# Where the first weights are made: moving early work between VectorE, GpSimd and the load queue in a retention and two-layer kernel

## The chip, the cores and the metric

The kernel runs on one core of a Trainium2 chip. The metric is the device time of one execution in microseconds (us). Three runs of the kernel before gave 1457.69 us as their median (1457.62 to 1459.07).

## The reference, cut to what matters

```python
# q, k, v: (8 batches, 8 heads, 576 positions, 64)
scores = matmul(q, k.T) / sqrt(64)
ret = scores * Dmat              # gamma_h ** (i - j) where i >= j, else 0
x = matmul(ret, v)               # -> x: (4608 tokens, 512)
h = maximum(maximum(x @ w1, x @ w2), x @ w3)     # 512 -> 768
x = h @ w_out                                    # 768 -> 512
h = x @ w_in                                     # 512 -> 2048
out = (h * clip(h + 3, 0, 6) / 6) @ w_out2       # 2048 -> 512
```

All matrices come in as float32; the weights are handed to the core as the bits of float64.

## The kernel before, in words

**Units.** Retention is done in 32 units, a unit being one batch and one pair of heads; it is computed in chunks of 64 positions. A unit's input is one tile `raw` (or `room`, the same tile in another pool) of 128 x 2304 floats with four sections of 576 columns: `Z0`, `Z1` (queries and keys transposed), `VS1`, `VS0` (values and keys of the two heads). The first eight units (two batches) run ahead of everything else; in the program they are `us[0]` to `us[7]`, in the text units one to eight. Each goes through these steps:

- `prepare` scales the keys of section VS1 by their decay: for units one to four on ScalarE (L373) with one piece on VectorE or GpSimd (L365), from unit five on as one instruction of GpSimd (L365).
- `outers` (L382) and `scores` (L284) are matmuls of 64 x 64 blocks; a half of the array works on each head. `copied` (L399, ScalarE) and `carry` (L405) put the running state where the values can use it.
- `mask` (L426, VectorE) multiplies the scores by a table that `fill` (L351) made; there is one table per pair of heads, so four calls of `fill`.
- `values` (L320) are 16 matmuls; `values_rest` (L434, VectorE) multiplies them by the second table, and `finish` writes them as two parts, high (L333, ScalarE cast to fp32r) and low (L336, full minus high, on GpSimd or VectorE). In before, the low parts of units three to seven are not issued where they arise but put on a list `low` and issued from the loop's sixth pass on.

**Weights.** A weight tile of the first layer (24 of them, in the order `order_a`) is loaded as 128 x 512 int64 (`ws`, L100), and turned into fp32 and two fp32r parts in stages: `begin` (L113 and L114 on VectorE), `rise` (L121 and L124 on ScalarE), `join` (L132 and L134 on VectorE, then the product L136 on GpSimd; it also loads the next tile), `end` (high part, L147 on ScalarE) and `lows` (low part, L153 on VectorE). `step` does `end` of one tile, `begin` of another, `join` of a third and `lows`, in this order. Every projection `block(t, f, j)` (tokens of batch t, column tile f, matrix j) is 12 matmuls L525, L526, L527 in turn: for each of four slices of the weight tile high x high, high x low, low x high. So its first two matmuls need the tile's high part, the third its low part. `block(t, f)` without j is the second matrix of that layer.

**Order.** All is in program order per engine (`manual_schedule`): nothing is reordered, and an instruction that waits holds up all that is behind it on its engine. The eight units run in a loop in which pass i does the values of unit i+1 and the outers of the unit two further on; the steps of the weights are put between by the pass number. Then `plan` runs the blocks of the first two batches in pairs, (0,0,0), (1,0,0), (0,0,1), (1,0,1), (0,0,2), (1,0,2), (0,1,0), ..., and after each block a rule decides whether a `step` follows. Loads are issued from SyncE's queue in program order (`load_raw`, L245, two or three transfers per unit; `fetch`, L100). TensorE first runs 40 matmuls of zeros (L596), which nothing reads.

Of the kernel before, what the change touches and what calls it, by code (L numbers as in the profile page):

```python
# [37 lines left out]
def retention_moe_moe2(ctx: ExitStack, tc, raw, w_a, w_b, factors, masks, out):  # L38
# [198 lines left out]
    def load_raw(i, room=None):  # L237
        if i >= len(units) or i in raws:
            return
        b, hp = units[i]  # L240
        t = room if room is not None else at.tile([P, RAW], F32, tag="raw", bufs=3, name="raw")
        raws[i] = t

        def part(c0, c1):
            nc.sync.dma_start(out=t[:, c0:c1], in_=raw[b, hp, :, c0:c1])  # L245

        if i:
            part(VS1, RAW)
            part(Z0, VS1)
            return  # L250
        part(VS1, VS0)
        part(VS0, RAW)
        part(Z0, VS1)
# [6 lines left out]
            k = raws[i][:, VS1:VS0]  # L260
            nc.scalar.mul(k, k, kdec_sb[:, units[i][1], NC:])

    xs, low = {}, []
    banks = [ps_at.tile([P, 512], F32, name=f"at{n}") for n in range(2)]

    class Unit:
# [63 lines left out]
        def finish(self, eng=None):  # L330
            b, hp, y = self.b, self.hp, self.y
            hi, lo = xs[b][:, 0, hp, :], xs[b][:, 1, hp, :]
            nc.scalar.copy(hi, y[:, :TB])  # L333

            def rest(eng):
                eng.tensor_tensor(out=lo, in0=y[:, :TB], in1=f32(hi), op=ALU.subtract)  # L336

            if eng is low:
                low.append(lambda: rest(nc.gpsimd))
            elif eng is not None:  # L340
                rest(eng)
            else:
                late.append(lambda: rest(nc.vector))
                late.append(lambda: nc.sync.dma_start(out=xe_d[:, hp, b * C:(b + 1) * C], in_=y[:, TB:]))
# [3 lines left out]
    def fill(hp):  # L348

        for n, one in enumerate((mask_sb, qdec_sb)):  # L350
            nc.vector.tensor_tensor(  # L351
                out=tables[hp][:, n].rearrange("p (c s) -> p c s", s=C),
                in0=one[:, hp, None, :].to_broadcast([P, NC - 1, C]),
                in1=powers_sb[:, hp, n, :NC - 1, None].to_broadcast([P, NC - 1, C]), op=ALU.mult)

    class Summed(Unit):
# [75 lines left out]
        def values_rest(self):  # L432
            self.y = (rooms if self.hp % 2 else at).tile([P, S], F32, tag="yr", bufs=2, name="yr")
            nc.vector.tensor_tensor(  # L434
                out=self.y[:, :TB], in0=self.ps[1], in1=tables[self.hp][:, 1], op=ALU.mult)
            self.finish(nc.gpsimd if self.i < 2 else low if self.i < 2 * HP - 1 else nc.vector)

        def put_end(self):
            t = raws[self.i].rearrange("p (k s) -> p k s", s=S)
# [133 lines left out]
    with tc.manual_schedule():  # L573
# [6 lines left out]
        load_raw(1)  # L580
        load_raw(2, room())
        load_raw(3, room())
        wa.fetch(1)
        load_raw(4, room())
        wa.fetch(1)
        load_raw(5)
# [5 lines left out]
        pairs = [banks, spare[:2], spare[2:],  # L592
                 [ps_mm.tile([P, 512], F32, tag="mm", name="mm") for n in range(2)]]
        us = [Summed(i, pairs[i % HP if i < 2 * HP - 1 else 0]) for i in range(2 * HP)]
        for n in range(40):
            nc.tensor.matmul(spare[3][halves[n % 2], :C], lhsT=zeros[halves[n % 2], :], rhs=zeros[halves[n % 2], :],  # L596
                             start=True, stop=True)
        us[0].prepare()
        fill(0)
        fill(1)  # L600
# [1 line left out]
        us[0].all_scores()  # L602
        us[0].copied(0)
        us[1].prepare()
        us[0].join()
        us[0].mask()
        us[1].outers()
# [5 lines left out]
        us[0].values_rest()  # L613
        us[1].mask()
        us[1].join()
        fill(3)

        def block(t, f, j=None):

# [9 lines left out]
        for i, u in enumerate(us):  # L629
            one, two, three = (us[i + n] if i + n < len(us) else None for n in (1, 2, 3))  # L630
            if i:
                u.values_mm()
            u.put_end()
            if i == 0:
                load_raw(6)
            if i == 2:
                load_raw(7, room())
                wa.fetch(1)
            if one and one.i >= HP:
                one.carry()  # L640
            if three:
                three.prepare()
            if i == 0:
                ends.fill()
            if two:
                two.outers(True)
            if i:
                u.values_rest()
            begun, parts = wa.begun, wa.end() if i in (4, 6) else []
            if 1 < i < 6:  # L650
                wa.begin() if i != 4 else None
                if wa.joined < begun:
                    wa.join()
            wa.lows(parts)
            if two:
                two.copied(0)
                wa.rise()
                two.mask()
                if two.i < HP:
                    two.join()  # L660
            if i >= HP + 1:
                for n in range(2 if i < 2 * HP - 1 else len(low)):
                    low.pop(0)()
            if i == 2 * HP - 2:
                block(0, 0, 0)
        load_raw(8)
        load_raw(9)
        rooms.release()
# [10 lines left out]
        plan += [(0, f, 0), (1, f, 0), (0, f, 1), (1, f, 1), (0, f, 2), (0, f - 1), (0, f), (1, f, 2)]  # L679
        plan += [(1, g) for g in range(f)]  # L680
        decay(2 * HP)
        base = 2 * HP
        side = {(1, 1, 1): [(lambda k: ends.scores(), 0)], (1, 2, 0): [(lambda k: ends.values(), 0)],
                (1, f, 0): [(visit, 0)], (0, f, 1): [(ready, 0)], (1, f, 1): [(rest, 0)]}
        for n, (a, b) in enumerate(zip([(0, f - 1), (1, f, 2), (1, 1), (1, 3)], [(0, f), (1, 0), (1, 2), (1, 4)])):
# [2 lines left out]
        for n, blk in enumerate(plan):  # L688
            if n:
                block(*blk)  # L690
            if wa.ended < NA and n % 3 != 1 and blk != (1, 1, 1):
                wa.step()
                if wa.ended == NA - 1:
                    wb.fetch(2)
# [329 lines left out]
```

## Time and profile before

| | us |
|---|---|
| median of three runs | 1457.69 |
| the profiled execution | 1459.42 |
| its span, first to last instruction | 1457.6 |
| TensorE busy | 1442.6 |
| VectorE busy | 894.7 |

The page gives each engine's busy time over the span and in 40 slices; the timeline gives single instructions with the idle time before them and what ended it. The part of the program that the diff touches ends at some 160 us of the span; behind it the remaining batches and the second layer run with TensorE busy for nine tenths or more of every slice up to the last. The reading below is of the first 160 us.

### The profile page before, as it was taken

Reading aid. Unit: us, or ns where it says so; the run is one execution under the profiler, and the core shown is the slowest. Engines: PE = TensorE matmul, PEld = TensorE weight load, DVE = VectorE, ACT = ScalarE, POOL = GpSimd, SP = SyncE. Lnnn points to the kernel's source line nnn. Section 1 sums busy time; section 2 is a strip of 40 time slices with the busy share of each in tenths; the row PEclk is TensorE's granted clock in tenths of the full one; section 3 lists DMA queues with packets and bytes.
Section 4 is the critical chain, followed back from the end, with each engine's and each line's share of the span. In section 5 each row is a group of like instructions: output and inputs, shape, how many; then the busy total and the mean of one; then the engine's idle time right before and its main releaser. Section 6 shows DMA issues by size and latency. Waiting matters only on the chain.

```text
span 1457.6 us, 24529 instructions
## 1 busy us (share of the span) xinstructions
PE 1442.6 (99%) x9760; PEld 1248.5 (86%) x9760; DVE 894.7 (61%) x1851; ACT 448.2 (31%) x838; POOL 163.4 (11%) x124
## 2 busy tenths in 40 slices
PE   8999999999999999999999999999999999999998
PEld 7887888888888888888898899899898898898897
DVE  7888878777778752214446646555654655566544
ACT  5544233434343311112222322232232222223222
POOL 4434013333333300000000000000000000000000
PEclk9999999999999999999999999999999999999999
DMA  8434345656565501064643363364445436444431
GB/s 341 155 108 145 134 145 195 224 205 233 198 224 193 199 9 57 2 215 139 224 128 112 117 210 115 101 224 116 116 146 179 116 87 239 116 115 167 116 101 44
DMA packets 94402, 219.02 MB, mean 150 GB/s; under 512 B 14032, under 2 KB 17232, under 8 KB 94288
## 3 DMA queue, kind: packets, MB, share of 16 engines
q1 hardware_dynamic: 93920, 216.96, 45.2%
q8 instruction: 78, 1.28, 0.4%
q10 hardware_dynamic: 368, 0.48, 0.1%
q14 instruction: 36, 0.29, 0.1%
HBM read 174.42 MB, written 42.99 MB: 149 GB/s over the span
## 4 chain that ended last, share of the span: by engine, by line
PE 92%; DVE 5%; ACT 1%; issue 1%; DMA 0%; POOL 0%; ACTq 0%; DVEq 0%; POOLq 0%
PE mm L525 18%; PE mm L527 17%; PE mm L526 17%; PE o L865 5%; PE o L866 5%; PE o L864 5%; PE o L525 3%; PE o L527 3%; PE o L526 3%; PE p L866 3%; PE p L865 3%; PE p L864 3%; PE mm L320 2%; PE at L284 1%; DVE xf L755 1%; DVE g L821 1%
## 5 line engine op out<-in xcount | busy, mean ns | idle before, releaser
L53 ACT CAST gp<-g 128x384 fp32r<-128x384 f32 x192 | 98.6, 513 | 336.5 <-DVE g L821 334.0
L525 PE MATMUL mm<-x,w 128*128 128x512 f32 x468 | 184.6, 394 | 0.1
L527 PE MATMUL mm<-x,w 128*128 128x512 f32 x468 | 182.6, 390 | 0.2
L526 PE MATMUL mm<-x,w 128*128 128x512 f32 x468 | 182.3, 389 | 0.0
L54 DVE TENSOR_TENSOR gp<-g,gp 128x384 fp32r<-128x384 f32 x192 | 107.2, 558 | 112.0 <-ACT gp L53 112.0
L828 DVE TENSOR_TENSOR cc<-mm,c 128x384 f32<-128x384 f32 x142 | 78.7, 554 | 137.2 <-PE mm L527 95.4
L542 DVE TENSOR_TENSOR t<-mm,t 128x512 f32<-128x512 f32 x108 | 74.1, 686 | 136.6 <-PE mm L527 136.5
L865 PE MATMUL o<-w,gp 128*128 128x512 f32 x384 | 151.1, 394 | 0.0
L866 PE MATMUL o<-w,gp 128*128 128x512 f32 x384 | 150.5, 392 | 0.0
L864 PE MATMUL o<-w,gp 128*128 128x512 f32 x384 | 150.1, 391 | 0.0
L525 PE MATMUL mm<-T,wq 128*128 128x384 f32 x382 | 129.6, 339 | 0.9
L833 ACT COPY c<-mm 128x384 f32<-128x384 f32 x143 | 68.5, 479 | 197.1 <-PE mm L527 197.1
L527 PE MATMUL mm<-T,wq 128*128 128x384 f32 x382 | 128.8, 337 | 0.0
L526 PE MATMUL mm<-T,wq 128*128 128x384 f32 x382 | 128.5, 336 | 0.0
L136 POOL TENSOR_TENSOR wf<-wf,wp 128x512 f32<-128x512 f32 x56 | 83.3, 1489 | 317.3 <-DVE wp L134 300.0
L525 PEld LDWEIGHTS mm<-x,w 128*128 128x128 f32 x468 | 87.8, 188 | 19.7 <-DVE t L542 0.5
L527 PEld LDWEIGHTS mm<-x,w 128*128 128x128 f32 x468 | 87.8, 188 | 19.5 <-DVE w L153 1.0
L526 PEld LDWEIGHTS mm<-x,w 128*128 128x128 f32 x468 | 87.9, 188 | 17.9 <-DVE x L336 0.2
L53 ACT CAST h<-t 128x512 fp32r<-128x512 f32 x54 | 33.6, 622 | 205.5 <-DVE t L542 199.9
L525 PE MATMUL mm<-B,wq 128*128 128x384 f32 x286 | 96.4, 337 | 0.0
L527 PE MATMUL mm<-B,wq 128*128 128x384 f32 x286 | 96.3, 337 | 0.0
L526 PE MATMUL mm<-B,wq 128*128 128x384 f32 x286 | 96.1, 336 | 0.0
(182 smaller groups left out, 2917.9 us busy)
## 6 DMA issues: line engine op xcount, KB each, us to landing
wq<-wqd SPq DMA_DIRECT2D x336, 256.0 KB, 3.1
raw<-in_raw SPq DMA_DIRECT2D x55, 576.0 KB, 5.4
ws<-in_w_b SPq DMA_DIRECT2D x32, 512.0 KB, 4.8
ws<-in_w_a SPq DMA_DIRECT2D x24, 512.0 KB, 3.5
wqd<-y SPq DMA_DIRECT2D x24, 512.0 KB, 2.7
x2d<-y SPq DMA_DIRECT2D x18, 512.0 KB, 3.4
wod<-y SPq DMA_DIRECT2D x16, 512.0 KB, 3.2
w<-wod SPq DMA_DIRECT2D x16, 512.0 KB, 4.4
```

The source lines that it names most:

```text
L53: nc.scalar.copy(hi, full)
L54: late.append(lambda: nc.vector.tensor_tensor(out=lo, in0=full, in1=f32(hi), op=ALU.subtract))
L136: nc.gpsimd.tensor_tensor(out=frac, in0=frac, in1=f32(power), op=ALU.mult)
L525: nc.tensor.matmul(ps, lhsT=wh, rhs=xh, start=first, stop=False, skip_group_check=read)
L526: nc.tensor.matmul(ps, lhsT=wh, rhs=xl, start=False, stop=False, skip_group_check=read)
L527: nc.tensor.matmul(ps, lhsT=wl, rhs=xh, start=False, stop=last, skip_group_check=read)
L542: nc.vector.tensor_tensor(out=tmp[t, f], in0=ps, in1=tmp[t, f], op=ALU.max)
L828: nc.vector.tensor_tensor(out=c, in0=a, in1=b, op=ALU.add)
L833: nc.scalar.copy(c, ps)
L864: nc.tensor.matmul(outs[s], lhsT=gh, rhs=wo[f][:, 0, :], start=start, stop=False)
L865: nc.tensor.matmul(outs[s], lhsT=gh, rhs=wo[f][:, 1, :], start=False, stop=False)
L866: nc.tensor.matmul(outs[s], lhsT=gl, rhs=wo[f][:, 0, :], start=False, stop=stop)
```

## The change

Seven things are changed, all in the first part of the program but for the split of the loads.

1. Six matmuls of zeros with 512 columns take the place of 40 with 64.
2. `fill(3)` is issued earlier, behind `us[1].prepare()`, and on GpSimd instead of VectorE.
3. The low parts of the units are issued where they arise, on GpSimd; the list `low` is gone.
4. Unit eight's `prepare` is issued one pass earlier.
5. The first weight is loaded behind unit five instead of ahead of it, and the two next behind unit eight instead of one ahead of unit six and one behind unit eight.
6. From unit five on, an input is loaded in four transfers of 576 columns (VS1, VS0, Z0, Z1) instead of two of 1152.
7. The weights' first stages are tied to other passes of the loop, and in `plan` a step follows every block that is not in `calm`, instead of two of three.

```diff
+        if i > HP - 1:
+            for c in (VS1, VS0, Z0, Z1):
+                part(c, c + S)
+            return
         if i:
             part(VS1, RAW)
             part(Z0, VS1)
...
         for n, one in enumerate((mask_sb, qdec_sb)):
-            nc.vector.tensor_tensor(
+            (nc.vector if hp < HP - 1 else nc.gpsimd).tensor_tensor(
...
-            self.finish(nc.gpsimd if self.i < 2 else low if self.i < 2 * HP - 1 else nc.vector)
+            self.finish(nc.gpsimd if self.i < 2 * HP - 1 else nc.vector)
...
-        wa.fetch(1)
         load_raw(4, room())
         wa.fetch(1)
         load_raw(5)
...
-        for n in range(40):
-            nc.tensor.matmul(spare[3][halves[n % 2], :C], lhsT=zeros[halves[n % 2], :], rhs=zeros[halves[n % 2], :],
-                             start=True, stop=True)
+        for n in range(6):
+            own = halves[n % 2]
+            nc.tensor.matmul(spare[3][own, :].rearrange("p (n d) -> p n d", d=C), lhsT=zeros[own, :],
+                             rhs=zeros[own, None, :].to_broadcast([D, 512 // C, C]), start=True, stop=True)
...
         us[1].prepare()
+        fill(3)
...
-        fill(3)
...
                 load_raw(7, room())
-                wa.fetch(1)
+                wa.fetch(2)
...
-            if three:
+            if three and i < HP:
                 three.prepare()
+            if i == HP - 1:
+                us[2 * HP - 1].prepare()
...
-            begun, parts = wa.begun, wa.end() if i in (4, 6) else []
-            if 1 < i < 6:
-                wa.begin() if i != 4 else None
-                if wa.joined < begun:
-                    wa.join()
-            wa.lows(parts)
             if two:
                 two.copied(0)
-                wa.rise()
                 two.mask()
                 if two.i < HP:
                     two.join()
-            if i >= HP + 1:
-                for n in range(2 if i < 2 * HP - 1 else len(low)):
-                    low.pop(0)()
+            if i == HP - 1:
+                wa.begin()
+                wa.rise()
+            if i == HP:
+                wa.join()
+            if i == HP + 1:
+                parts = wa.end()
+                wa.begin()
+                wa.rise()
+                wa.lows(parts)
             if i == 2 * HP - 2:
                 block(0, 0, 0)
+                wa.join()
...
-        base = 2 * HP
+        base, calm = 2 * HP, [(1, g, j) for g in range(F1) for j in (0, 2)] + [(1, 1, 1)]
...
-            if wa.ended < NA and n % 3 != 1 and blk != (1, 1, 1):
+            if wa.ended < NA and blk not in calm:
                 wa.step()
```

VectorE, from the maximum of block (0,0,1) on, in before. `t_760` is the running maximum of batch 0, `t_819` of batch 1; `ws`, `wp`, `wf` are stages of a weight, and `w_835` is the tile of the third weight, which block (0,0,2) multiplies by.

```order
L542 TENSOR_TENSOR t_760<-mm_821,t_760 128x512
L113 TENSOR_SCALAR wp_837<-ws_643 128x512
L114 TENSOR_SCALAR wf_838<-ws_643 128x512
L132 SCALAR_TENSOR_TENSOR wf_796<-ws_573,wf_796 128x512
L134 SCALAR_TENSOR_TENSOR wp_795<-ws_573,wp_795 128x512
L153 TENSOR_TENSOR w_835<-wf_707,w_835 128x512
L542 TENSOR_TENSOR t_819<-mm_849,t_819 128x512
```

The same place in the kernel after, with line numbers higher by two and other tile numbers: `t_721` and `t_786` are the maxima of batch 0 and 1, `w_827` the third weight's tile.

```order
L544 TENSOR_TENSOR t_721<-mm_788,t_721 128x512
L113 TENSOR_SCALAR wp_802<-ws_611 128x512
L114 TENSOR_SCALAR wf_803<-ws_611 128x512
L132 SCALAR_TENSOR_TENSOR wf_767<-ws_435,wf_767 128x512
L134 SCALAR_TENSOR_TENSOR wp_766<-ws_435,wp_766 128x512
L544 TENSOR_TENSOR t_786<-mm_813,t_786 128x512
L113 TENSOR_SCALAR wp_829<-ws_726 128x512
L114 TENSOR_SCALAR wf_830<-ws_726 128x512
L132 SCALAR_TENSOR_TENSOR wf_803<-ws_611,wf_803 128x512
L134 SCALAR_TENSOR_TENSOR wp_802<-ws_611,wp_802 128x512
L153 TENSOR_TENSOR w_827<-wf_767,w_827 128x512
```

The low part of the third weight stood ahead of batch 1's maximum (block (1,0,1)) and now stands behind it, and the join of the same weight (L132, L134 on `wf_767`), which stood ahead of batch 0's maximum, now stands behind that.

VectorE in before, from the maximum of block (0,1,2) (`t_938`) on. `t_967` is batch 1's maximum, `w_1064` the tile of the eighth weight, which block (0,2,0) multiplies by.

```order
L542 TENSOR_TENSOR t_938<-mm_1031,t_938 128x512
L54 TENSOR_TENSOR h_1045<-t_938,h_1045 128x512
L542 TENSOR_TENSOR t_967<-mm_1047,t_967 128x512
L113 TENSOR_SCALAR wp_1066<-ws_951 128x512
L114 TENSOR_SCALAR wf_1067<-ws_951 128x512
L132 SCALAR_TENSOR_TENSOR wf_986<-ws_921,wf_986 128x512
L134 SCALAR_TENSOR_TENSOR wp_985<-ws_921,wp_985 128x512
L153 TENSOR_TENSOR w_1064<-wf_943,w_1064 128x512
L54 TENSOR_TENSOR h_1062<-t_967,h_1062 128x512
```

And in the kernel after, from the low part of the seventh weight (`w_1011`) on, the eighth weight's tile being `w_1059` and the two maxima `t_902` and `t_931`.

```order
L153 TENSOR_TENSOR w_1011<-wf_907,w_1011 128x512
L54 TENSOR_TENSOR h_1009<-t_902,h_1009 128x512
L544 TENSOR_TENSOR t_931<-mm_1025,t_931 128x512
L54 TENSOR_TENSOR h_1040<-t_931,h_1040 128x512
L113 TENSOR_SCALAR wp_1061<-ws_958 128x512
L114 TENSOR_SCALAR wf_1062<-ws_958 128x512
L132 SCALAR_TENSOR_TENSOR wf_1014<-ws_915,wf_1014 128x512
L134 SCALAR_TENSOR_TENSOR wp_1013<-ws_915,wp_1013 128x512
L153 TENSOR_TENSOR w_1059<-wf_950,w_1059 128x512
```

A step (five instructions, L113 to L153) now stands ahead of batch 1's maximum, and the step that ends with the eighth weight's low part now stands behind the low part of batch 1's hidden tile (L54).

SyncE's queue in before, from unit four's input (`room_143`) on; `raw_153`, `raw_332` and `room_458` are units six to eight, each `ws` is a weight.

```order
L245 DMA room_143<-in_raw 128x1152 x2
L100 DMA ws_146<-in_w_a 128x512
L245 DMA room_148<-in_raw 128x1152 x2
L100 DMA ws_151<-in_w_a 128x512
L245 DMA raw_153<-in_raw 128x1152 x2
L245 DMA raw_332<-in_raw 128x1152 x2
L245 DMA room_458<-in_raw 128x1152 x2
L100 DMA ws_461<-in_w_a 128x512
```

The same in the kernel after, where `room_146`, `raw_153`, `raw_300` and `room_428` are units five to eight.

```order
L245 DMA room_143<-in_raw 128x1152 x2
L245 DMA room_146<-in_raw 128x576 x4
L100 DMA ws_151<-in_w_a 128x512
L245 DMA raw_153<-in_raw 128x576 x4
L245 DMA raw_300<-in_raw 128x576 x4
L245 DMA room_428<-in_raw 128x576 x4
L100 DMA ws_433<-in_w_a 128x512
L100 DMA ws_435<-in_w_a 128x512
```

One weight fewer stands ahead of each of units five to eight.

## Rows read from the trace of the kernel before

The spans of GpSimd's instructions are rough, as the page says; PE is TensorE's matmuls, PEld its weight loads, DVE VectorE, ACT ScalarE, POOL GpSimd. A float32 matmul of a unit shows as two records on each of PE and PEld.

**Rows 1.** Page: busy us (share of the span) xinstructions of each engine.
```profile
PE 1442.6 (99%) x9760; PEld 1248.5 (86%) x9760; DVE 894.7 (61%) x1851; ACT 448.2 (31%) x838; POOL 163.4 (11%) x124
```

**Rows 2.** Stretches (us): busy us (xinstructions) by engine, PEclk, DMA share, GB/s.
```profile
31.50:34.90 3.40, 3.40 (x59) 2.60 (x57) 2.14 (x4) 1.77 (x4) 1.77 (x2) 0.50 0.39 137
...
40.70:160.00 119.30, 117.50 (x728) 95.30 (x729) 98.40 (x175) 55.31 (x97) 38.18 (x24) 1.00 0.35 113
```

**Rows 3.** Timeline of TensorE: start us, us, engine line op names xcount [idle before].
```profile
0.98 3.99 PE L596 MATMUL o<-zeros 64*64 64x64 f32 x80 [0.98 <-DVE rebias L587]
...
5.52 2.17 PE L382 MATMUL at<-raw 64*64 64x256 f32 x26 [0.55 <-ACT raw L373]
...
9.02 2.63 PE L382 MATMUL o<-raw 64*64 64x256 f32 x32 [0.44 <-ACT raw L373]
```

**Rows 4.** Timeline of TensorE and its weight loads, three waits named issue.
```profile
18.26 0.13 PEld L284 LDWEIGHTS mm<-room 64*64 64x64 f32 x1 [0.38 <-issue]
...
24.45 0.27 PE L284 MATMUL at<-room 64*64 64x64 f32 x2 [1.12 <-issue]
...
30.72 1.03 PE L320 MATMUL at<-room 128*64 128x64 f32 x25 [1.90 <-issue]
```

**Rows 5.** Page, DMA queue of instructions: packets, MB, share of 16 engines.
```profile
q8 instruction: 78, 1.28, 0.4%
```

**Rows 6.** DMA between 9 and 31 us: packets, MB, mean rate.
```profile
DMA packets 2172, 8.72 MB, mean 396 GB/s; under 512 B 248, under 2 KB 248, under 8 KB 2167
```

**Rows 7.** Timeline of TensorE: units five to eight, then the first projection.
```profile
26.04 0.43 PE L382 MATMUL o<-raw 64*64 64x256 f32 x2
...
28.37 0.45 PE L320 MATMUL at<-room 128*64 128x64 f32 x7
...
31.69 0.69 PE L382 MATMUL o<-raw 64*64 64x256 f32 x2
...
35.57 1.15 PE L320 MATMUL o<-raw 128*64 128x64 f32 x32
...
39.00 1.15 PE L320 MATMUL o<-raw 128*64 128x64 f32 x32
...
40.66 0.50 PE L525 MATMUL mm<-x,w 128*128 128x512 f32 x1
```

**Rows 8.** Timeline of VectorE: a mask of unit eight, then one weight step.
```profile
39.82 1.41 DVE L426 TENSOR_TENSOR room<-at,w 64x512 f32<-64x512 f32 x2
...
50.49 0.69 DVE L542 TENSOR_TENSOR t<-mm,t 128x512 f32<-128x512 f32 x1 [1.69 <-PE mm L527]
...
51.10 0.42 DVE L113 TENSOR_SCALAR wp<-ws 128x512 uint32<-128x512 uint32 x1
...
51.77 0.69 DVE L132 SCALAR_TENSOR_TENSOR wf<-ws,wf 128x512 f32<-128x512 uint32 x1
...
52.98 0.68 DVE L153 TENSOR_TENSOR w<-wf,w 128x512 fp32r<-128x512 f32 x1
```

**Rows 9.** Timeline of GpSimd and ScalarE: the weight of L132 above, multiplied and rounded.
```profile
53.14 1.68 POOL L136 TENSOR_TENSOR wf<-wf,wp 128x512 f32<-128x512 f32 x1 [2.96 <-DVE wp L134]
...
54.85 0.62 ACT L147 CAST w<-wf 128x512 fp32r<-128x512 f32 x1 [2.05 <-POOL wf L136]
```

**Rows 10.** Timeline of TensorE: a matmul before a wait, and two that waited.
```profile
53.24 0.39 PE L526 MATMUL mm<-x,w 128*128 128x512 f32 x1
...
53.71 0.50 PE L527 MATMUL mm<-x,w 128*128 128x512 f32 x1
...
129.24 0.50 PE L525 MATMUL mm<-x,v 128*128 128x512 f32 x1 [1.56 <-ACT t L540]
```

**Rows 11.** Timeline of GpSimd and VectorE: two instructions side by side.
```profile
61.84 1.61 POOL L136 TENSOR_TENSOR wf<-wf,wp 128x512 f32<-128x512 f32 x1 [3.45 <-DVE wp L134]
...
62.22 1.78 DVE L54 TENSOR_TENSOR h<-t,h 128x512 fp32r<-128x512 f32 x1
```

**Rows 12.** Timeline of VectorE: the fourth call of fill.
```profile
16.04 1.70 DVE L351 TENSOR_TENSOR w<-masks_sb,factors_sb 128x512 f32<-128x512 f32 x2
```

More of the change, by code (lines that the diff above doesn't have):

```diff
@@ L261, in decay @@
             nc.scalar.mul(k, k, kdec_sb[:, units[i][1], NC:])
-    xs, low = {}, []
+    xs = {}
     banks = [ps_at.tile([P, 512], F32, name=f"at{n}") for n in range(2)]
@@ L336, in rest @@
                 eng.tensor_tensor(out=lo, in0=y[:, :TB], in1=f32(hi), op=ALU.subtract)
-            if eng is low:
-                low.append(lambda: rest(nc.gpsimd))
-            elif eng is not None:
+            if eng is not None:
                 rest(eng)
```

## The prediction, made before the changed kernel had run

> **What bounds the kernel now.** I read the page's busy times first: TensorE is busy for 1442.6 of 1457.6 us [rows 1], so a change pays only where TensorE waits, and costs only where it makes it wait. The stretches come next: behind 40.7 us TensorE was busy for 117.50 of 119.30 us, so 1.8 us of idle time is all that the projections of the first two batches have to give, while VectorE was busy for 98.40 us there and has little room to catch up [rows 2]. Then I read the timeline of the first 40 us. Three waits of TensorE there are ended by nothing that the profile shows (issue): 0.38, 1.12 and 1.90 us, in all 3.40, ending at 18.26, 24.45 and 30.72 us [rows 4]. Behind the last the granted clock was 0.50 for 3.4 us, the lower of the two levels (1.2 of 2.4 GHz) [rows 2]: unit seven's outers and scores took 31.69 to 35.57, 3.88 us, where unit six's took 26.04 to 28.37, 2.33 us [rows 7]. That price is 1.55 us.
>
> The three waits look like the instruction stream. The queue of instructions brought 78 packets [rows 5] for 2 x 9760 records of TensorE [rows 1], 250 each. A unit is 48 matmuls of two loads and two products, 192 records. Between the waits lie 250 records as well (from unit four's scores to unit five's scores, from there into unit five's values), and they end 6.2 us apart. So while data moved at 396 GB/s [rows 6], TensorE got one packet per 6.2 us; at unit six's pace, 128 records in 2.33 us [rows 7], 250 take 4.5.
>
> The Trainium skill speaks against this reading: its page "Runtime: NRT & Kernel Launch", section "Instruction fetch mechanics", says that the stream comes in blocks of 256 instructions and that crossing a block's edge costs one small DMA step, "mostly hidden". The block's size agrees with 250; hidden the edges are not here, if the 3.40 us are theirs. By that rule fewer records would gain nothing, which is a rival below.
>
> **The change part by part.** The sum is made on the profiled execution, 1459.42 us.
>
> *Zeros.* 40 matmuls show as 80 + 80 records [rows 3], so six leave 24: 136 fewer, and every edge moves 0.7 units further into the program. They stream 6 x 512 columns instead of 40 x 64, 1.2 times as many; 3.99 us becomes 4.8 if the clock rises no sooner, and they end at 5.8 instead of 5.0, when unit one's outers waited until 5.52 for ScalarE [rows 3]. Cost 0 to 0.3 us, and unit two, which starts at 9.02 behind its own data, hides it. I take 0.
>
> *Edges after.* The first edge now falls into unit two's outers, started at 9.02 [rows 3]. At 6.2 us per packet the next can be passed at 15.2, 21.4, 27.6 and 33.8: hardly a wait at 15.2, then one in unit three's values, one early in unit six's outers, one late in unit seven's. Behind 33.8 come 30% of unit seven (0.7), unit six's values (35.57 to 36.67 or so, 1.1) and unit eight's outers and scores (2.33). So unit eight's scores end, call it S, at 37.9; in before S is 39.00 [rows 7]. Its inputs come sooner (one weight less ahead of it: 0.52 MB at 396 GB/s, 1.3 us [rows 6]), so the last packet may find emptier queues; I take 1.7 us gained. Bounds: 5.0 if the 3.40 and the 1.55 all go, -0.3 if they all stay and the zeros are late.
>
> *Four transfers, fill(3), low parts, unit eight's prepare.* The bytes and rate are the same; the keys' section arrives first, but no unit from five on waits for data in before. VectorE loses 1.70 us of fill ahead of unit three's mask [rows 12], GpSimd gains it while it waits. No cost and no gain of their own: the stream sets the pace there. If it doesn't, they are part of the 5.0.
>
> *Weights.* Here I find the loss. In before two weights are finished when the plan begins; after, one is, and the second's join is issued behind block (0,0,0).
> (a) Block (0,0,0) starts at S + 1.66 in before [rows 7]; its third matmul, two of 0.23 later, finds the low part long done. After, VectorE does unit eight's mask (1.41), two instructions of begin (0.67 from start to start) and only then the low part (0.68) [rows 8]: S + 2.9, and 0.3 more beside GpSimd's low parts. The third matmul runs at S + 3.2, not S + 2.1: +1.1 (bounds 0.7 and 1.7).
> (b) Block (0,0,1): its low part stands behind unit eight's values and low part and a begin; 0 to 0.7, I take 0.3.
> (c) Block (0,0,2). Let T be the end of block (0,0,1). A block is 12 x 0.23 = 2.77 us, so (0,0,2) wants its high part at T + 2.77 and its low part at T + 3.23. After, the join stands behind (0,0,1)'s maximum. From the start of such a maximum to that of L132 it is 1.28 us [rows 8], from L132 to the end of the high part 3.70 (51.77 to 55.47, through GpSimd's 1.68) [rows 8, 9]. The last matmul's 0.39 [rows 10] reaches 0.16 past T, and I give the maximum 0.25 to start; so the high part is ready at T + 5.2. The low part stands behind (1,0,1)'s maximum, which cannot start before T + 3.0, and from such a maximum to the low part's end it is 3.17 (50.49 to 53.66) [rows 8]: T + 6.2. Beside a product of GpSimd, VectorE's instruction took 1.78 instead of 0.68 [rows 11], which makes it up to T + 7.0. TensorE waits 3.0 to 3.8 us, most of it ahead of the first matmul; I take 3.4.
> (d) Block (0,2,0). Batch 1's maximum, the cast (0.62), batch 1's low part (0.6) and a whole step now stand between the end of block (1,1,2) and the eighth weight's low part: 0.25 + 0.69 + 0.62 + 0.6 + 2.5 = 4.7 us (durations of [rows 8, 9]), and the third matmul behind block (0,0) wants it after 3.23. 1.5 us if VectorE is free when (1,1,2) ends, 3.3 if the step ahead of the maximum and GpSimd's lock hold it for 1.8; I take 2.5, as VectorE is busy for 82% there [rows 2].
> (e) The blocks between, where a step follows each of them: 0 to 1.2, I take 0.6.
> What goes: the wait at 53.71 (0.47 since the matmul before instead of 0.23 [rows 10], with two more like it at 79.88 and 111.02) and 1.56 at 129.24, behind ScalarE's copy [rows 10]: 2.3 in all, if none comes back.
>
> Sum: 1.1 + 0.3 + 3.4 + 2.5 + 0.6 - 2.3 = 5.6 (bounds 2.9 and 10), less 1.7: 3.9 us over 1459.42, 1463.3. The profiled execution stands 1.73 over the median of the runs. Two of these gave 1457.62 and 1457.69 and one 1459.07, as if two had no stretch at half clock; then nothing of the 1.55 is left to gain in them and their sum comes out at 1463.3 too. If the 1.73 is the profile's own, it is 1461.6. I say 1462.5.
>
> **The rivals.** *The clock falls in the new waits.* A wait of 1.90 was followed by half clock, waits of 1.12 and 1.56 were not [rows 2, 4, 10]. (c) and (d) are longer waits, each broken by two matmuls. Half clock for 3.4 us costs 1.7: once 1464.2, twice 1465.9. For it speaks the length; against it, that TensorE is dense on both sides.
>
> *The stream is not the cause* (the page's rule): the 3.40 us stay where they are, the gain is 0, 1464.2.
>
> *Gain and loss cancel.* The gain reaches its bound of 5.0, or the losses are at theirs (2.9): 1459.2 to 1460.1. For it speaks that the loads come sooner and VectorE is freer in the first 40 us; against it, that the edges move and do not go.
>
> *Faster.* The place is the stream: transfers of half the size may let an instruction packet in sooner. From 15.2 on each edge would then be passed as early as TensorE comes to it, S would be 34.0, and VectorE, given 5 us more before the plan, would have the third weight's join behind it at (0,0,1). It decides from the point where the waits in (0,0,2) and (0,2,0) stay under 2 us together: 1459.42 + 1.1 + 2.0 - 2.3 - 5.0 = 1455.2. Against it stands the order: the low part in (c) is behind (1,0,1)'s maximum however early S is.
>
> **How the numbers follow.** The forecast has 0.46 (own range 1460.7 to 1465), the clock 0.13, the page's rule 0.05: slower by over 0.2%, 2.9 us, which is about what a measurement of this kernel can tell from no change, 0.64. Cancelling has 0.25 and is within 0.2%; faster has 0.11. The range runs from between the two last, 1457.0, to the clock's second fall and a little of the bound of 10, 1466.5.
>
> **What would show it.** Right: TensorE waits of 2 us or more ahead of the first matmul of (0,0,2) and of 1 to 3 us in (0,2,0), ended by the high part (ScalarE) and the low part (VectorE) of the weight; no wait of 1.5 us at some 129; issue waits that are fewer and end 6.2 us apart at other places; S at 37 to 38. Wrong: no wait over 1 us in these two blocks; S at 34 or below (the stream was freed) or at 39 (it was not the stream); a time of 1460 or less.

## The result, and the profile after

| | median us | runs | against before |
|---|---|---|---|
| before | 1458.38 (1457.62 to 1459.23) | 4 | |
| after | 1475.43 (1473.64 to 1476.52) | 4 | 1.0113, 95% interval 1.0097 to 1.0129 |

The change made the kernel slower by 1.1%: 17.1 us by the medians, 16.5 by the ratio. I had said 1462.5 us with a range to 1466.5: the sign was right, the size and the range were wrong. The profiled execution took 1474.89 us, its span 1472.7 us, 15.1 more than before.

The page of the kernel after, busy time and number of instructions by engine; it answers to [rows 1]:

```profile
PE 1449.4 (98%) x9692; PEld 1248.3 (85%) x9692; DVE 892.6 (61%) x1849; ACT 448.5 (30%) x838; POOL 163.1 (11%) x126
```

TensorE has 68 records fewer and is busy for 6.8 us more, so some of the same matmuls ran slower. The stretches say where (columns as in [rows 2]; the first two rows are its stretches, the last three are those in which the granted clock was at its lower level):

```profile
31.50:34.90 3.40, 2.71 (x82) 2.11 (x74) 1.98 (x5) 3.26 (x8) 0.44 (x1) 1.00 0.06 18
40.70:160.00 119.30, 109.62 (x526) 85.69 (x526) 91.00 (x152) 53.93 (x95) 37.38 (x24) 0.96 0.40 129
58.75:62.17 3.42, 3.42 (x10) 2.68 (x9) 0.21 (x1) 0.00 (x0) 0.29 (x1) 0.50 0.37 138
89.47:92.89 3.42, 2.83 (x7) 2.25 (x8) 3.42 (x5) 0.00 (x0) 1.59 (x1) 0.50 0.51 153
123.60:127.02 3.42, 3.42 (x10) 2.68 (x9) 1.48 (x3) 1.24 (x3) 1.59 (x1) 0.50 0.33 110
```

Behind 40.7 us TensorE is idle for 9.7 us of 119.3 instead of 1.8, and the mean clock is 0.96 instead of 1.00. The fall at 31.5 us is gone; three new ones, of 3.4 us each, lie among the projections. The waits of TensorE between 40 and 165 us, by what ended them (total, times, longest, in us), after:

```profile
PE mm L529 <- DVE w L153: 3.9, 4, 2.0
PE mm L527 <- ACT w L147: 3.6, 3, 1.9
PE mm L527 <- ACT t L542: 3.2, 2, 2.4
```

and before:

```profile
PE mm L525 <- ACT t L540: 1.6, 1, 1.6
```

High parts of weights (L147) and low parts (L153) are new here; the copy of a projection (L540, now L542) had made the one wait of before [rows 10]. The timeline of TensorE after shows the three places that are followed by half clock: block (0,0,2), block (0,2,0) and block (1,3,1), and a last wait (start us, us, instruction [idle before]):

```profile
53.86 0.39 PE L529 MATMUL mm<-x,w 128*128 128x512 f32 x1
56.17 0.50 PE L527 MATMUL mm<-x,w 128*128 128x512 f32 x1 [1.93 <-ACT w L147]
56.51 0.40 PE L528 MATMUL mm<-x,w 128*128 128x512 f32 x1
57.95 0.50 PE L529 MATMUL mm<-x,w 128*128 128x512 f32 x1 [1.04 <-DVE w L153]
...
59.15 0.63 PE L527 MATMUL mm<-x,w 128*128 128x512 f32 x1
59.58 0.63 PE L528 MATMUL mm<-x,w 128*128 128x512 f32 x1
...
87.38 0.50 PE L527 MATMUL mm<-x,w 128*128 128x512 f32 x1 [0.90 <-ACT w L147]
87.71 0.40 PE L528 MATMUL mm<-x,w 128*128 128x512 f32 x1
90.06 0.80 PE L529 MATMUL mm<-x,w 128*128 128x512 f32 x1 [1.95 <-DVE w L153]
...
122.54 0.50 PE L527 MATMUL mm<-x,w 128*128 128x512 f32 x1 [2.39 <-ACT t L542]
...
162.24 0.50 PE L527 MATMUL mm<-x,v 128*128 128x512 f32 x1 [0.85 <-ACT t L542]
```

Matmuls start 0.23 us apart at full clock and 0.43 apart (59.15 to 59.58) at half. From the first projection matmul to the visit at 160.12 us (145.80 before) I added up what each start-to-start step takes over 0.23: waits 17.7 us against 6.8 before (units' matmuls in between count in both), steps at half clock 4.2 against none. Together 15.1, of a shift that grows by 15.4 there. The first block starts at 39.57 instead of 40.66, which takes 1.1 off, and the wait of 0.85 at 162.24 puts most of that on again. That makes 14.3 and 0.85 of the 15.1 us, so the rest of the program adds nothing that shows.

### The profile page after: what moved, and what is told of

The parts are those of the page before. It is cut to its first block, busy times and chain, and to the rows that moved or that the text cites. A ratio compares the mean times of both kernels' runs of the same rounds, so it can differ in the third digit from the quotient of the medians.

```text
span 1472.7 us, 24487 instructions
## 1 busy us (share of the span) xinstructions
PE 1449.4 (98%) x9692; PEld 1248.3 (85%) x9692; DVE 892.6 (61%) x1849; ACT 448.5 (30%) x838; POOL 163.1 (11%) x126
## 4 chain that ended last, share of the span: by engine, by line
PE 86%; DVE 8%; DMA 3%; ACT 1%; issue 1%; POOL 0%; SPq 0%; ACTq 0%; DVEq 0%; POOLq 0%
PE mm L527 17%; PE mm L529 16%; PE mm L528 16%; PE o L870 5%; PE o L871 5%; PE o L869 5%; PE o L527 3%; PE o L529 3%; PE o L528 3%; PE p L871 3%; PE p L870 3%; PE p L869 3%; PE mm L324 2%; PE at L288 1%; DVE xf L760 1%; DMA raw<-in_raw 1%
## 5 line engine op out<-in xcount | busy, mean ns | idle before, releaser
L527 PE MATMUL mm<-x,w 128*128 128x512 f32 x468 | 186.7, 399 | 6.0 <-ACT w L147 3.6
L529 PE MATMUL mm<-x,w 128*128 128x512 f32 x468 | 185.2, 396 | 4.0 <-DVE w L153 3.9
L528 PE MATMUL mm<-x,w 128*128 128x512 f32 x468 | 184.0, 393 | 0.0
L54 DVE TENSOR_TENSOR gp<-g,gp 128x384 fp32r<-128x384 f32 x192 | 107.2, 558 | 111.9 <-ACT gp L53 111.9
L544 DVE TENSOR_TENSOR t<-mm,t 128x512 f32<-128x512 f32 x108 | 74.1, 686 | 144.4 <-PE mm L529 144.4
L527 PEld LDWEIGHTS mm<-x,w 128*128 128x128 f32 x468 | 89.0, 190 | 27.1 <-ACT w L147 5.3
L529 PEld LDWEIGHTS mm<-x,w 128*128 128x128 f32 x468 | 88.9, 190 | 25.6 <-DVE w L153 6.8
L528 PEld LDWEIGHTS mm<-x,w 128*128 128x128 f32 x468 | 88.9, 190 | 18.3 <-DVE x L340 0.2
```

The lines of the kernel that those rows point to most:

```text
L54: late.append(lambda: nc.vector.tensor_tensor(out=lo, in0=full, in1=f32(hi), op=ALU.subtract))
L527: nc.tensor.matmul(ps, lhsT=wh, rhs=xh, start=first, stop=False, skip_group_check=read)
L528: nc.tensor.matmul(ps, lhsT=wh, rhs=xl, start=False, stop=False, skip_group_check=read)
L529: nc.tensor.matmul(ps, lhsT=wl, rhs=xh, start=False, stop=last, skip_group_check=read)
L544: nc.vector.tensor_tensor(out=tmp[t, f], in0=ps, in1=tmp[t, f], op=ALU.max)
```

## The experiments

Theory W: the schedule of the weights alone makes the loss. Rivals are named in the expectations. All ratios are against the kernel before on the same chip, with their 95% intervals.

### Which part of the change

Each of the first four kernels has one part, or all but one; a1 and a2 split items 5 and 7 from the rest, a3 is item 6, a4 item 1.

```diff
# a1: before, with items 5 and 7 alone       # a2: after, with items 5 and 7 taken back
# a3: before, with
+        if i > HP - 1:
+            for c in (VS1, VS0, Z0, Z1):
+                part(c, c + S)
# a4: before, with six wide matmuls of zeros for 40
```

> The kernel before with nothing of the change but its weights' schedule: fetches later, steps in other passes of the loop over units, steps left out behind other blocks. Theory W (the schedule of the weights alone makes the whole loss, and the rest of the change gains about 1 us): 1474 to 1478 us, with three falls of the granted clock to 0.50 between 50 and 130 us. Rival R (the loss comes mostly from the other parts, transfers in quarters and decays on GpSimd, which make the same schedule too late): 1461 to 1466 us and at most one fall. Rival P (the predicted sum holds without the startup gain): 1464 to 1465 us.

> The changed kernel with the weights' schedule of the kernel before put back in all its parts (fetches, passes, blocks with a step); wide zeros, quarters, tables and decays on GpSimd stay. Theory W: 1456.5 to 1458.5 us, the first block some 1 us earlier than before and no later waits of over 1 us but the one near 129 us. Rival R: 1466 to 1472 us, since what made the loss is still there.

> The kernel before with units five to eight loaded in four transfers each and nothing else. Theory W: 1457.4 to 1459.0 us, within 0.1% of before, since TensorE in 9 to 38 us is held by the landing of whole units, not of parts. Rival R: 1460 us or more, since 8 more transfers stand ahead of the weights' in SP's queue.

> The kernel before with 6 wide products of zeros in place of 40 narrow ones and nothing else. Theory W: 1457.4 to 1458.8 us; the waits called issue move by 34 instructions' time into other groups, and the first block starts 0 to 1 us earlier. Rival (the waits of the instruction stream are a matter of what they stand in, and the fall of the clock near 31.5 us with it): the fall at 31.5 us goes and the time is 1456.0 to 1457.3 us.

| | median us | ratio |
|---|---|---|
| a1 weights' schedule alone | 1478.17 | 1.0128 (1.0115 to 1.0142) |
| a2 all but it | 1459.00 | 0.9995 (0.9986 to 1.0004) |
| a3 transfers alone | 1458.95 | 0.9996 (0.9987 to 1.0005) |
| a4 zeros alone | 1458.98 | 0.9993 (0.9984 to 1.0002) |

W holds: a1 has the loss (0.2 us above W's range; its trace even has four falls, that at 31.6 us among them). The rest is worth nothing that can be measured: a2 stands above W's range, on a chip where before took 1459.56, and the gain of 1 us that W gave the rest is not seen. Nor does a2's first block start 1 us earlier, as W had it: in its trace it starts at 40.46, 0.2 us earlier. In a2 to a4 the fall near 31.5 us was absent from the profiled execution, and still the times stand within 0.1% of before. The rival in a4's expectation is not settled: a4 lies above both ranges, and 0.9993 with its interval holds a gain of 0.16% as well as none. Where the waits called issue stand changes the time by no more than that. In a4 they ended at 16.09, 22.11 and 28.32 us, moved as reckoned and not gone.

### Which piece of the weights' schedule

Three pieces can be put back singly: the fetches (item 5), the passes of the loop, and the rule for steps in `plan`.

```diff
# b1: after, with the old rule
-            if wa.ended < NA and blk not in calm:
+            if wa.ended < NA and n % 3 != 1 and blk != (1, 1, 1):
# b2: after, with the old fetches and passes   # d2: old fetches alone   # f1: old passes alone
```

The theories O and F that d2's expectation names are those of d1, in the next part.

> The changed kernel with the old rule for steps between blocks (every block but each third one), its late fetches and passes kept. Theory L (the passes and fetches before the first block make the loss; by block (0,2,0) both rules have done 8 steps): 1470 to 1476 us, waits at (0,0,1), (0,0,2) as in the changed kernel. Rival Q (the new rule, with three steps in a row and then two pauses, makes it): 1460 to 1464 us.

> The changed kernel with the old fetches and passes in the loop over units, and the new rule for steps between blocks kept. Theory L: 1458 to 1462 us, no wait over 1 us before 100 us. Rival Q: 1468 to 1474 us, with the waits at (0,2,0) and (1,3,1) as in the changed kernel.

> The changed kernel with the weights' fetches back at their early places in SP's queue and everything else kept, its later steps included. Theory O: the steps are as late as in the changed kernel, 1473 to 1478 us. Rival F: 1460 to 1468 us.

> The changed kernel with the weights' steps in the loop's passes as in the kernel before, but the fetches left late (the second weight lands near 31.5 us, while its first step stands in the pass that begins some 7 us earlier). Theory T (fetch and steps belong together): VectorE waits for that landing with unit five's or six's masks behind it, TensorE loses 2 to 6 us ahead of the first block, and 1464 to 1470 us result. Rival O (only the steps' places matter): 1460 to 1463 us, as with early fetches.

| new rule | late fetches | early fetches |
|---|---|---|
| new passes | 1.0113 (after) | 1.0101 (1.0085 to 1.0116) (d2) |
| old passes | 1.0056 (1.0043 to 1.0070) (f1) | 1.0020 (1.0011 to 1.0030) (b2) |

With the old rule: new passes and late fetches 1.0137 (1.0120 to 1.0154) (b1), old passes and early fetches 0.9995 (a2). So the passes are the larger part, 0.6 to 0.8% (8 to 12 us); early fetches alone give back nothing that the intervals separate. The new rule costs 0.25% where the steps are early (b2 against a2); where they are late it seems to save as much (b1 against after), but there the intervals overlap. b1 took 1477.94 us, 2 us above its range, on theory L's side all the same; b2 (1461.94), d2 (1475.02) and f1 (1467.06) lie inside the ranges of L, O and T.

f1 shows why fetches and passes go together. Its timeline of VectorE (begin of the second weight, and what stood behind it):

```profile
31.48 0.46 DVE L113 TENSOR_SCALAR wp<-ws 128x512 uint32<-128x512 uint32 x1 [2.46 <-DMA ws<-in_w_a]
...
33.51 1.41 DVE L428 TENSOR_TENSOR raw<-o,w 64x512 f32<-64x512 f32 x2
```

VectorE waited 2.46 us for the weight's landing, with a unit's mask behind it, and the first block began near 42.7 us instead of 40.66. That is 2.1 of the 8 us that f1 loses. Behind the first block its trace has waits of 4.8 us for copies and maxima (L542, L544), of which b2 has 3.0, and two falls of the clock, at 22.81 and 135.45; up to 165 us b2 has none.

### One step more ahead of the first block

d1 ends the second weight and begins and joins the third ahead of block (0,0,0), as in before, with late fetches. It put each low part behind the next weight's join, and its third matmul waited 2.8 us for that; e3 has them the other way round.

```diff
-            if i == HP + 1:
+            if i in (HP + 1, HP + 2):
                 parts = wa.end()
                 wa.begin()
                 wa.rise()
+                wa.join()              # e3: behind wa.lows(parts)
                 wa.lows(parts)
```

> The changed kernel with one more of the weights' steps ahead of the first block: the second weight ended and the third begun and joined there, as in the kernel before, with the late fetches kept. Theory O (the loss is that every weight stands one step later): no wait over 1 us at (0,0,1), (0,0,2) and (0,2,0), no fall of the clock there, 1459 to 1463 us. Rival F (the late fetches make the steps late, wherever they stand): TensorE waits as much ahead of the first block instead, 1467 to 1475 us.

> The changed kernel with one more weights' step ahead of the first block, as in an earlier run, but with each low part ahead of the next weight's join on VectorE. Theory O: the wait of 2.9 us in the first block goes, with its fall of the clock; no wait over 1 us up to (0,2,0); what may stay are waits for GpSimd's multiplication near 117 and 138 us: 1462 to 1467 us. Rival F (the late fetches): as before, 1469 us or more.

d1 took 1471.09 us, 1.0068 (1.0055 to 1.0081), e3 1469.16, 1.0069 (1.0055 to 1.0083): both of theory O's ranges were missed. Rival F's numbers fit, its mechanism does not: TensorE did not wait ahead of the first block, which began at 39.34 in e3. In e3 the waits for weights' parts are gone up to (0,2,0) but for 0.5 us, and another came (timelines of TensorE and ScalarE of e3):

```profile
48.59 0.53 PE L527 MATMUL mm<-x,w 128*128 128x512 f32 x1 [2.11 <-ACT x L337]
```
```profile
43.60 0.62 ACT L147 CAST w<-wf 128x512 fp32r<-128x512 f32 x1 [0.15 <-POOL wf L136]
44.12 0.72 ACT L121 ACTIVATE wp<-wp,rebias 128x512 int32<-128x512 int32 x1
45.32 0.64 ACT L124 ACTIVATE wf<-wf 128x512 f32<-128x512 uint32 x1 [0.48 <-DVE wf L114]
...
47.92 0.62 ACT L337 CAST x<-yr 128x512 fp32r<-128x512 f32 x1 [1.19 <-DVE yr L436]
```

The step now stands ahead of unit eight's parts, which block (1,0,0) needs: the wait changed its owner, and the clock fell behind it again. A weights' step fits ahead of the first block only where there is room for it, in the earlier passes, and there only if the tile has landed.

### The falls of the clock, and GpSimd beside VectorE

The edits are shown condensed; for b4 the condition is `self is wa` alone. b3 lets TensorE multiply zeros in the three waits; b4 moves the product of each weight from GpSimd to VectorE; e1 that of three weights; e2 is e1 with zeros in the two waits left.

```diff
+        ahead, amid = {(0,0,2): (2,1), (0,2,0): (1,2), (1,3,1): (2,0)}.get((t, f, j), (0, 0))
+        keep_busy(ahead)           # wide products of zeros into banks[1], nobody reads them
...
+        keep_busy(amid)            # ahead of the first block's third matmul
...
-            nc.gpsimd.tensor_tensor(out=frac, in0=frac, in1=f32(power), op=ALU.mult)
+            (nc.vector if self is wa and self.joined in (9, 14, 19) else nc.gpsimd).tensor_tensor(...)
```

> The changed kernel with 3 wide products of zeros of 0.98 us each put into each of the waits at (0,0,2) and (0,2,0), and 2 into that at (1,3,1), so that TensorE works where it waited. Theory C (each fall of the clock to 0.50 follows the wait ahead of it, and costs 1.5 to 1.8 us): the three falls go and the time is 1469 to 1471.5 us, about 5 us less than the changed kernel. Rival D (the falls are not made by these waits, or they move to other places): three or more falls remain, 1474 to 1478 us.

> The changed kernel with the last multiplication of each of the 24 up and down weights' steps on VectorE (about 0.7 us) in place of GpSimd (1.6 us, 3.5 us where it runs beside VectorE). Theory X (the chain from fetch to the weight's parts is what the waits are): each chain is about 1 us shorter or 2.5 where GpSimd was held up, waits of (0,0,1), (0,0,2) and (0,2,0) fall by about 1 us each, the wait at (1,3,1) goes with its fall of the clock: 1464 to 1470 us. Rival V (VectorE's own queue sets the steps): waits stay or grow by VectorE's additional 16 us in 120 us, 1474 to 1480 us.

> The changed kernel with the last multiplication of three of the 24 weights (9th, 14th, 19th, those that took 3.48 us beside VectorE's work in one trace or another) on VectorE. Theory G (GpSimd and VectorE in each other's way make the wait at (1,3,1)): that wait of 2.55 us goes with its fall of the clock (some 1.6 us), the others stay: 1470.5 to 1472.5 us. Rival H (it is late anyway): 1474 to 1477 us.

> The same, with 3 wide products of zeros in each of the waits at (0,0,2) and (0,2,0) as well. Theory C (a fall of the clock costs about 1.6 us, by the matmuls' 0.43 us instead of 0.23 us over 3.4 us): no fall is left, 2.5 to 3.3 us less than the run with the three alone. Rival D (the granted clock falls at some other place instead): less than 1 us between the two.

| | median us (lowest to highest) | ratio |
|---|---|---|
| b3 | 1472.98 (1472.59 to 1473.54) | 1.0097 (1.0082 to 1.0112) |
| b4 | 1472.74 (1472.03 to 1474.02) | 1.0096 (1.0081 to 1.0111) |
| e1 | 1471.47 (1471.03 to 1476.98) | 1.0094 (1.0079 to 1.0108) |
| e2 | 1470.11 (1469.78 to 1470.38) | 1.0075 (1.0062 to 1.0088) |

The stretch from 40 to 165 us, in the order after, b3, e1, e2 (columns as in [rows 2]):

```profile
40.00:165.00 125.00, 114.08 (x608) 89.11 (x607) 94.81 (x161) 56.41 (x99) 38.43 (x24) 0.96 0.38 124
```
```profile
40.00:165.00 125.00, 118.57 (x635) 90.01 (x634) 95.85 (x167) 56.52 (x99) 40.29 (x24) 0.99 0.37 124
```
```profile
40.00:165.00 125.00, 115.30 (x616) 89.71 (x617) 96.55 (x171) 56.71 (x99) 32.14 (x21) 0.97 0.37 124
```
```profile
40.00:165.00 125.00, 119.21 (x643) 90.77 (x642) 98.59 (x177) 56.61 (x99) 32.17 (x21) 1.00 0.37 124
```

None of the three falls is left in b3. By itself that shows little, for falls come and go: in d2's trace, with waits of 0.87 and 1.95 us at (0,2,0) as after and no zeros, the granted clock was 1.00 behind them, and behind a wait of 2.65 us at 142.28 too. Nor had b3 a wait to fill at (1,3,1): that wait turned up at (1,4,1), 2.6 us, with a fall of its own. So b3 gave 2.4 us, and not the 5 of theory C.

The test is e2 against e1. With TensorE at work in its waits there is no fall in this stretch of e2's trace, and its five runs lie within 0.6 us, all below the fastest of e1, whose runs spread over 6 with mean clocks of 0.993 to 0.999. The two profiled executions, none against two falls, are 3.33 us apart (1469.78 and 1473.11). Over all runs the falls that e1 still has cost 1.4 us by the medians, between the two theories' ranges, and 2.8 by the ratios, which weigh the runs' means and lie in C's range.

The wait at (1,3,1) is two engines in each other's way. GpSimd and VectorE after, then the same pair of instructions in a3, where that wait did not come:

```profile
110.59 1.60 POOL L136 TENSOR_TENSOR wf<-wf,wp 128x512 f32<-128x512 f32 x1 [1.97 <-DVE wp L134]
116.74 4.71 POOL L136 TENSOR_TENSOR wf<-wf,wp 128x512 f32<-128x512 f32 x2 [4.55 <-DVE wp L134]
```
```profile
116.51 0.69 DVE L153 TENSOR_TENSOR w<-wf,w 128x512 fp32r<-128x512 f32 x1
117.12 0.42 DVE L113 TENSOR_SCALAR wp<-ws 128x512 uint32<-128x512 uint32 x1
```
```profile
122.66 1.60 POOL L136 TENSOR_TENSOR wf<-wf,wp 128x512 f32<-128x512 f32 x1 [4.55 <-DVE wp L134]
```
```profile
122.43 0.68 DVE L153 TENSOR_TENSOR v<-wf,v 128x512 fp32r<-128x512 f32 x1
123.03 1.51 DVE L113 TENSOR_SCALAR wp<-ws 128x512 uint32<-128x512 uint32 x1
```

In a3 GpSimd's product took 1.60 us and L113 1.51 instead of 0.42; after, VectorE ran on through four instructions more, up to 119.08, and the first of GpSimd's two ended at 120.22, 3.48 us behind its start. The starts do not tell which of the two will be held: in both traces the product begins 0.23 us behind L153 and 0.37 or 0.38 ahead of L113. Up to 165 us all the traces together have 27 such pairs in which L113 was held and 15 in which the product was, with these starts the same to 0.04 us. Then ScalarE's high part at 120.26 had waited 3.45 us for it, with the copy L542 of block (1,3,0) behind it, and TensorE wants that copy's bank. The Trainium skill's page "SBUF — State Buffer", section "Who interferes with whom", says that the two engines share a pair of ports, given for a whole instruction to the one that issues first, while the other blocks; these rows agree that one of the two is held, and which issued first they do not show. So the wait can come or stay away in one and the same kernel. e1 took it away and came 2.8 us under after by the ratios (0.0019 of 1458), inside its range; the two intervals overlap, so that gain is likely and not shown. b4, which moves all 24, did no better and lies between its theories' ranges: its waits for low parts came to 7.7 us, where after has 3.9 and e1 4.5. VectorE has 16 us more to do there, which would explain it.

Has before lost that wait as well, when two of its products are moved? And is a kernel with the rest of the change then faster than both?

```diff
# e4: before, c2: a2, both with            # c1: a2, with all 24 on VectorE
+            (nc.vector if self is wa and self.joined in (19, 23) else nc.gpsimd).tensor_tensor(...)
```

> The kernel before with the last multiplication of its 19th and 23rd weight on VectorE, nothing else. Theory G: the wait of 1.56 us at 129.24 us goes: 0.10 to 0.15% under the kernel before. Rival H: within 0.05% of it.

> The kernel with all of the change but the weights' schedule (it ran in 1459.0 us), with the last multiplication of two of the 24 weights, the 19th and 23rd, on VectorE instead of GpSimd. In its trace and in that of before the 19th took 3.48 us beside VectorE's work instead of 1.6 us and the matmuls at (1,4,1) then waited 1.56 to 1.95 us. Theory G (the two engines in each other's way make that wait): the wait goes and the time is 1456.0 to 1457.8 us. Rival H (the step itself is late there): the wait stays, 1458.5 to 1460 us.

> The kernel with all of the change but the weights' schedule, with the last multiplication of all 24 weights on VectorE. Theory G: the wait at (1,4,1) goes as well, and VectorE's 16 us more in 120 us are hidden: 1456 to 1458 us. Rival V (VectorE's queue sets the steps): new waits for its low parts of 0.5 to 3 us at several blocks, 1460 to 1468 us.

c2 took 1458.91 us, 0.9988 (0.9979 to 0.9996); e4 1458.44, 0.9998 (0.9989 to 1.0006); c1 1459.73, 0.9996 (0.9987 to 1.0005). Expected of c2 was 1456.0 to 1457.8, on a chip where before took 1460.76, and of e4 0.10 to 0.15% less; G's waits went, its gain didn't show in e4, whose time is that of rival H. In c1, between its two ranges, waits for low parts came, of 0.8 us at most. In c2 and e4 no wait of over 0.3 us is left between 41 and 165 us. c2 is the fastest that ran, by 0.12%, but e4, with the same edit on before, shows no gain, so I don't call the edit's gain shown. In a3, which leaves the weights as they were, the wait was absent as well: it may be that before has it in some executions only.

## Why the prediction was wrong, step by step

- *(c), right.* T, the end of (0,0,1), is 51.37: its last matmul starts at 51.14, 0.23 ahead. The high part of (0,0,2) was to be ready at T + 5.2, 56.6; the matmul started at 56.17. The low part was to end at T + 6.2 to T + 7.0, 57.6 to 58.4; the matmul started at 57.95. The loss is 3.3 us, start to start; I had 3.4.
- *(a), (d) and (e), right within their bounds or nearly.* (a): the third matmul ran at 40.79, S + 3.0 (S + 3.2 said), 0.65 us lost instead of 1.1. (d): 3.2 instead of 2.5. (e): one wait, before the matmul at 71.34, 0.55 us lost instead of 0.6.
- *(b), wrong.* 1.1 us instead of 0.3, outside 0 to 0.7. I followed the low part; the high part was later. Its product was ready at 45.29, but on ScalarE it stood behind the decay of unit nine, which waited for a load:

```profile
46.89 0.78 ACT L265 ACTIVATE raw<-raw,factors_sb 128x576 f32<-128x576 f32 x1 [0.97 <-DMA raw<-in_raw]
47.58 0.60 ACT L147 CAST w<-wf 128x512 fp32r<-128x512 f32 x1
```

- *The sum put the falls of the clock at nothing: the first of the two steps that failed.* I had them as a rival with 0.13, one or two, at 1.7 us. There were three, 4.2 us in all in the profiled execution (1.4 each on average), behind waits of 1.93 and 1.04, of 0.90 and 1.95, and of 2.39. I argued that TensorE is dense on both sides; so it was also ahead of the fall in [rows 2, 4], which stood behind a wait of 1.90.
- *"If none comes back": the second step that failed.* I took 2.3 us off for waits that go. The 1.56 of [rows 10] came back as 2.39 and with a fall, and 0.85 at 162.24 beside it; two small losses of 0.25 each stand at 83.43 and 103.47. The term came out at about +1.5 instead of -2.3. I had read that wait as one behind ScalarE's copy; what it stood on was GpSimd held up by VectorE, for which I had a row [rows 11] and charged nothing there. That it came back in this execution is in part chance, by the pairs above.
- *The startup gain, a size that did not count.* Timeline of TensorE after, as [rows 4] and the last two of [rows 7]:

```profile
21.80 0.68 PE L324 MATMUL o<-room 128*64 128x64 f32 x15 [1.61 <-issue]
...
27.67 0.32 PE L384 MATMUL o<-raw 64*64 64x192 f32 x1 [0.86 <-issue]
...
32.87 0.27 PE L288 MATMUL o<-raw 64*64 64x64 f32 x2 [0.53 <-issue]
...
37.77 1.15 PE L324 MATMUL o<-raw 128*64 128x64 f32 x32
...
39.57 0.50 PE L527 MATMUL mm<-x,w 128*128 128x512 f32 x1
```

S was 37.77 (37.9 said). The waits called issue ended at 21.80, 27.67 and 32.87 (21.4, 27.6 and 33.8 said), in unit three's values, unit six's outers and unit seven's, as said, 5.9 and 5.2 us apart; 3.00 us in all instead of 3.40. That they are the instruction stream's edges fits, and the traces hold more for it than I had read: in before, after, a2, a3 and a4 each of the three waits ends 1.2 to 1.6 us behind the end of a transfer on the queue of instructions (in before these end at 16.84, 23.01 and 29.36, the waits at 18.26, 24.45 and 30.72). No run takes the stream away. The 1.7 us for it were 1.1 in this trace; a4, whose first block starts as early (39.62), is not measurably faster than before (0.9984, 2.3 us under it, is the interval's end).

Net waits came to 11.7 us where the sum had 5.6, falls to 4.2 where it had none, the start to -1.1 where it had -1.7: 14.8 of the 15.1 us.

## What to carry to other kernels

When a step is moved later, count the waits it makes and then ask of each whether the clock falls behind it: here three places cost 9 us of waits and 4 of half clock, and zeros multiplied in two of the waits kept the mean clock at 0.999 or more in all five runs of e2. Follow both results of a moved step, on every engine's queue, for instructions ahead of it that wait for a load. A step can be taken back only together with its load: early load alone gave nothing, early step alone half, both nearly all.

## What the runs showed of the hardware

- The granted clock fell to 0.50, in the changed kernel for 3.4 us each time, also where the wait was broken by two matmuls (0.90 and 1.95 us at 87.38 and 90.06) and where matmuls ran at full clock between the wait and the fall (57.95 to 58.75). Whether it falls differs from run to run of one kernel: e1's five runs had mean clocks of 0.993 to 0.999 and took 1476.98 to 1471.03 us. In d2's trace it did not fall behind 0.87 and 1.95 us, nor behind 2.65.
- A product of GpSimd took 1.60 or 3.48 us, and an instruction of VectorE 0.42 or 1.51 us: one of the two was held by the other, in 42 pairs whose starts are the same to 0.04 us.
- The three early waits of TensorE that nothing else explains end 1.2 to 1.6 us behind a transfer on the queue of instructions, in five traces.
